# Moving elementwise work between engines, reordering the start, and placing buffers on the other side, in a forward-and-backward long-convolution kernel

## The chip, the cores and the metric

The kernel runs on one core of one Trainium2 chip. The metric is device time in microseconds (us), lower is better. Quoted times are medians over the runs of one kernel. The profile is one execution of the same program; its span is about two microseconds shorter than the times.

Names used below: PE is TensorE (matmuls), PEld its weight loads, DVE is VectorE, ACT is ScalarE, POOL is GpSimd, SP is SyncE, whose queue issues almost all transfers here.

## The reference

Four residual layers over x of 2048 x 512 (bf16), A, B, A, B, with shared weights, and then the gradient of all of it.

```python
def _A_ref(q, k, v, shift_k, ssm_k, ssm_D):
    k_shift = sum of 4 shifted copies of k, each times a column of shift_k   # (abridged)
    kv = k_shift * v
    kv_f, kf_f = rfft(kv padded to 2S), rfft(ssm_k padded to 2S)             # (abridged)
    y = irfft(kv_f * kf_f)[:S] + kv * ssm_D                                  # (abridged)
    return q * y
def _B_ref(x, w1, b1, w2, b2):
    h = _gelu(jnp.einsum("bsd,df->bsf", x, w1) + b1)                          # F = 1376, tanh GELU
    return jnp.einsum("bsf,fd->bsd", h, w2) + b2
x = A_q
x = x + _A_ref(_layernorm(x), A_k, A_v, ...)
x = x + _B_ref(_layernorm(x), B_w1, ...)
x = x + _A_ref(_layernorm(x), A_k, A_v, ...)
x = x + _B_ref(_layernorm(x), B_w1, ...)
# outputs: x, and the ten gradients of x for grad_out
```

The convolution result y depends only on k, v and the filters, so it is computed once and used by both A layers.

## The kernel before

The Fourier transforms are matmuls with cosine and sine blocks that the kernel generates itself. Its stages, in order, are these:

1. Generate the forward blocks (Fmat) and the inverse blocks (Imat) and store them.
2. Transform the filter h, form k_shift and kv, transform kv, multiply the spectra ("plain"), and transform back to y.
3. The forward layers. The dense layer works through four slices of 512 rows, twice (two B layers), with 11 chunks of up to 128 hidden columns in each slice.
4. The backward layers, twice: dense backward, weight gradients (dw2, then dw1), then the layer-norm backward of layer A.
5. gd (the gradient of ssm_D), the transform of gy, two spectral products ("conj", "conj_untwist"), two inverse transforms (gkv, then gh), and last gk and gw, the gradients of k and of shift_k.

The parts that the change and the argument touch, with cuts marked `...`:

```python
# --- start (setup_conv)
    with tc.tile_pool(name="gen_work", bufs=1) as gen_work, tc.tile_pool(name="gen_stage", bufs=3) as stage:
        gen_forward_blocks(nc, tc, gen_work, consts, dims, fdest)
        ...  # 32 stores Fmat <- Fblk
        for b in range(HT):
            for qc, qs in ((Q_ICE, Q_ISE), (Q_ICO, Q_ISO)):
                ...  # generate a pair of inverse blocks (stc, sts), store both to Imat
    ...
        for t in range(NT):
            nc.sync.dma_start_transpose(out=hT[:, t, :], in_=h_ap[0:D, t * P:(t + 1) * P])
    ...  # transform of h, then:
        with nc.allow_non_contiguous_dma(reason="tiny weight transpose"):
            nc.sync.dma_start(out=dram.WT[:, :], in_=W_ap.rearrange("d j -> j d"))
    ...
            eng = nc.gpsimd if (t % 2 == 0) else nc.vector      # k_shift: every second tile on POOL
            for j in range(4):
                ...
                    eng.tensor_tensor(out=tmp, in0=kj, in1=Wbc16[:, j, :], op=ALU.mult)
                    eng.tensor_tensor(out=ks, in0=ks, in1=tmp, op=ALU.add)

# --- spectral products
                nc.vector.scalar_tensor_tensor(out=t1, in0=Ar, scalar=sc, in1=Br, op0=ALU.mult, op1=ALU.mult)
                ...  # three more like it, then two tensor_tensor

# --- dense forward, one chunk (line numbers as in the profile)
            nc.scalar.activation(out=u, in_=ps, func=ACT.Identity, bias=w.b1col[...], scale=1.0)      # L634
            nc.gpsimd.tensor_tensor(out=wsq, in0=u, in1=u, op=ALU.mult)                               # L637
            nc.vector.tensor_scalar(out=tt, in0=wsq, scalar1=..., scalar2=..., ...)                   # L639
            nc.vector.tensor_tensor(out=arg, in0=tt, in1=u, op=ALU.mult)                              # L642
            nc.scalar.activation(out=sg, in_=arg, func=ACT.Sigmoid)                                   # L644
            nc.vector.tensor_tensor(out=hT_sl[0:fcs, c, :], in0=u, in1=sg, op=ALU.mult)               # L645
            nc.vector.tensor_scalar(out=tt, in0=tt, scalar1=3.0, ...)                                 # L646
            nc.gpsimd.tensor_tensor(out=wsq, in0=tt, in1=u, op=ALU.mult)                              # L648
            nc.vector.tensor_scalar(out=arg, in0=sg, scalar1=-1.0, scalar2=1.0, ...)                  # L649
            nc.gpsimd.tensor_tensor(out=arg, in0=arg, in1=wsq, op=ALU.mult)                           # L651
            nc.vector.scalar_tensor_tensor(out=gp, in0=arg, scalar=1.0, in1=sg, ...)                  # L653

# --- backward, weight gradients: pools opened on the same side as everything else
    with tc.tile_pool(name="bb_hm", bufs=3) as hm_pool, tc.tile_pool(name="bb_ev", bufs=2) as evp, ...
        ...  # per layer h_tm is loaded twice, 2 x 16 tiles of 344 KB
    with tc.tile_pool(name="bb_gm", bufs=3) as gm_pool, tc.tile_pool(name="bb_nm", bufs=3) as nm_pool, \
            tc.tile_pool(name="bb_ev1", bufs=2) as evp, ...

# --- the end: gk and gw, after both inverse transforms
        for t in range(NT):
            ...
                    nc.any.tensor_tensor(out=tmp, in0=gksj, in1=Wbc[:, j, :], op=ALU.mult)     # tmp, acc, Wbc in f32
                    nc.any.tensor_tensor(out=acc, in0=acc, in1=tmp, op=ALU.add)
                nc.any.tensor_tensor(out=prod, in0=gksj, in1=kt, op=ALU.mult)
                nc.tensor.matmul(psw[j], lhsT=consts.onescol, rhs=prod, start=(t == 0), stop=(t == NT - 1))
        ...
            with nc.allow_non_contiguous_dma(reason="tiny transposed store"):
                ...  # out4 stored element by element
```

## Time and profile before

The time before was 2176.45 us (four runs, 2174.79 to 2178.35). First come lines of the page of the kernel before: busy time of an engine (share of the span) and its instructions, and then the span cut in 40 slices of 54 us, each digit the busy share in tenths. "DMA" is the mean busy share of the 16 transfer engines.

```profile
PE 1134.6 (52%) x4992; PEld 463.8 (21%) x4992; DVE 1370.4 (63%) x2698; ACT 577.5 (27%) x947; POOL 395.1 (18%) x336
...
PE   0028009391655535666797572796550393049742
DVE  8447331778999999999474008671017718994296
POOL 0000550000677727777100000000000000000000
DMA  5721440703111121111344673347773426132242
```

No engine is the limit of the whole program: VectorE is busy 63% of it. Each stage has a limit of its own, and the rows of digits show the stages. TensorE does nothing in slices 0 and 1, has a hole in slices 4 and 5 while POOL works, and more holes in slices 24, 30, 31, 33 and 34. VectorE is at nine tenths or more in slices 10 to 18 (the dense forward). The transfer row is at 6 to 7 where VectorE is nearly idle (slices 22, 23, and 27 to 29: the weight gradients).

**The start.** The timeline of the SP queue of the kernel before over its first 150 us; columns are start, duration, engine, line, operation, out<-in, count:

```profile
0.74 0.82 SPq L342 DMA_DIRECT2D WT_d<-in_A_shift_k_dram  x1
1.62 30.15 SPq L541 DMA_DIRECT2D w_sb<-in_B_w_dram  x1
31.82 28.34 SPq L544 DMA_DIRECT2D w_sb<-in_B_w_dram  x11
60.28 21.28 SPq L291 DMA_DIRECT2D Fmat<-Fblk  x32
...
124.40 20.78 SPq L306 DMA_TRANSPOSE hT<-in_A_ssm_k_dram  x16
```

WT is a transposed store of two-byte elements. The 12 loads of w_sb behind it take until 60.16 us, so the stores of Fmat begin at 60.28 us and the transposing loads of h only at 124.40. The Trainium skill, "DMA: Bandwidth & Descriptors", Rules for kernel authors, says that a non-contiguous last dimension is lowered to one descriptor per element; the trace agrees, for its transfer records hold 2048 of two bytes, one for each of the 512 x 4 elements, that begin between 2.3 and 36.6 us. Why the loads of w_sb then take until 60 us is not shown.

**VectorE beside POOL.** The timeline of the kernel before inside one dense slice (VectorE and POOL lines picked out, same columns; brackets hold the idle time before and what ended it):

```profile
577.09 0.41 DVE L645 TENSOR_TENSOR hT_sl<-g_u,g_s 128x512 bf16<-128x512 bf16 x1
577.25 1.26 POOL L648 TENSOR_TENSOR g_w<-g_t,g_u 128x512 bf16<-128x512 bf16 x1 [0.83 <-DVE g_t L646]
577.43 1.24 DVE L649 TENSOR_SCALAR g_arg<-g_s 128x512 bf16<-128x512 bf16 x1
578.59 0.28 DVE L639 TENSOR_SCALAR g_t<-g_w 128x512 bf16<-128x512 bf16 x1
578.81 1.15 POOL L651 TENSOR_TENSOR g_arg<-g_arg,g_w 128x512 bf16<-128x512 bf16 x1 [0.30 <-DVE g_arg L649]
578.90 1.34 DVE L642 TENSOR_TENSOR g_arg<-g_t,g_u 128x512 bf16<-128x512 bf16 x1
```

L645, begun while POOL is idle, takes 0.41 us. L649, begun 0.18 us after a POOL operation, takes 1.24 us and ends 0.16 us after it; L639, begun when POOL is idle, takes 0.28. L642, the same kind of operation as L645, begins under L651 and takes 1.34. The VectorE operations here that begin under a POOL operation thus last until it is over. The groups of instructions of the kernel before (line, engine, operation, tiles, count, then busy us and mean ns, then idle time before and what ended it) hold the mixture of both kinds:

```profile
L653 DVE SCALAR_TENSOR_TENSOR g_gp<-g_arg,g_s 128x512 bf16<-128x512 bf16 (+1 forms) x88 | 97.7, 1114 | 14.1 <-POOL g_arg L651 14.1
L642 DVE TENSOR_TENSOR g_arg<-g_t,g_u 128x512 bf16<-128x512 bf16 (+1 forms) x88 | 82.7, 943 | 2.5 <-DVE g_t L646 0.3
L649 DVE TENSOR_SCALAR g_arg<-g_s 128x512 bf16<-128x512 bf16 (+1 forms) x88 | 77.3, 879 | 0.0
```

So L642 costs 943 ns on average instead of some 420. The Trainium skill, "SBUF — State Buffer", Terms, calls the port pair of VectorE and GpSimd an exclusive lock, where the loser "fully blocks". The timeline agrees with that rather than with shared bandwidth.

**Stages by window.** Busy time of each engine in stretches of the kernel before: a dense forward slice's worth, the first dw stage, the layer-norm backward after it, and the second pair. Columns: window, length, then busy us (instructions) of PE, PEld, DVE, ACT, POOL, then the granted clock of PE, DMA share, GB/s.

```profile
550.00:585.00 35.00, 19.65 (x84) 8.08 (x84) 31.52 (x52) 15.99 (x25) 25.41 (x22) 0.77 0.14 49
1176.00:1316.00 140.00, 95.14 (x367) 35.09 (x366) 2.21 (x4) 8.30 (x15) 0.00 (x0) 0.86 0.70 216
1316.00:1374.00 58.00, 12.10 (x35) 3.00 (x34) 54.40 (x134) 35.05 (x70) 0.00 (x0) 0.53 0.24 73
1477.00:1634.00 157.00, 96.56 (x368) 35.05 (x368) 14.86 (x23) 0.00 (x0) 0.00 (x0) 0.83 0.73 219
1634.00:1706.00 72.00, 0.00 (x0) 0.00 (x0) 61.10 (x146) 23.69 (x48) 0.00 (x0) 0.50 0.32 67
```

In the dense slice VectorE is busy 31.5 of 35 us. In the weight gradients TensorE is busy 95 of 140 us, the transfers 70%, and VectorE 2 us. Then VectorE is the busy engine, in the layer-norm backward: 54 of 58 us, and 61 of 72, with ScalarE at 35 and 24 us and TensorE at 12 and 0.

### The profile page before, as it was taken

How to read it: one execution, taken by the hardware profiler on the slowest of the kernel's cores; microseconds unless marked ns; L12 is line 12 of the kernel's file. 1: busy time of each engine (PE TensorE's matmuls, PEld its weight loads, DVE VectorE, ACT ScalarE, POOL GpSimd, SP SyncE). 2: the span in 40 equal slices, each digit the busy share in tenths (PEclk: the TensorE clock that was granted, in tenths of full speed). 3: DMA queues.
4: the chain of work that ended last, by engine and by line, in shares of the span. 5: the costliest groups of instructions: out<-in, count | busy, mean ns of one | idle time of the engine just before them, and what ended most of it. 6: DMA issues, size and time to landing. Idle time of an engine off the chain costs nothing.

```text
span 2175.8 us, 17475 instructions
## 1 busy us (share of the span) xinstructions
PE 1134.6 (52%) x4992; PEld 463.8 (21%) x4992; DVE 1370.4 (63%) x2698; ACT 577.5 (27%) x947; POOL 395.1 (18%) x336
## 2 busy tenths in 40 slices
PE   0028009391655535666797572796550393049742
PEld 0003004130222212222343220442220041014300
DVE  8447331778999999999474008671017718994296
ACT  8520003015455454333442005440003130001110
POOL 0000550000677727777100000000000000000000
PEclk9999559696767767666799886898885596569855
DMA  5721440703111121111344673347773426132242
GB/s 21 292 87 70 152 145 39 245 19 95 47 60 55 52 76 44 62 62 60 124 144 153 201 242 105 103 137 213 217 224 61 160 77 217 53 100 77 69 143 58
DMA packets 198639, 248.16 MB, mean 114 GB/s; under 512 B 35987, under 2 KB 146633, under 8 KB 197518
## 3 DMA queue, kind: packets, MB, share of 16 engines
q1 hardware_dynamic: 198542, 247.04, 36.8%
q8 instruction: 39, 0.64, 0.1%
q14 instruction: 58, 0.48, 0.1%
HBM read 152.24 MB, written 92.62 MB: 113 GB/s over the span
## 4 chain that ended last, share of the span: by engine, by line
DVE 41%; PE 27%; DMA 15%; issue 6%; POOL 4%; ACT 4%; SPq 3%; DVEq 0%; POOLq 0%; ACTq 0%
PE fwd_pss L179 4%; PE fwd_psc L176 4%; DVE g_gp L653 4%; PE gh_ps L785 3%; DMA dw_n<-n_d 3%; DVE g_arg L649 3%; DMA h_tm<-htm_d 3%; PE dw_ps L851 2%; DVE hT_sl L645 2%; PE dw_ps L822 2%; DMA sst<-Hspec_d 2%; PE inv_A L192 2%; DVE lb_junk L741 2%; PE inv_A L194 2%; DVE lb_tmp L747 2%
## 5 line engine op out<-in xcount | busy, mean ns | idle before, releaser
L660 PE MATMUL o_ps<-w_sb,hT_sl 128*128 128x512 bf16 (+1 forms) x352 | 136.1, 491 | 134.3 <-DVE hT_sl L645 132.6
L631 PE MATMUL z_ps<-nT,w_sb 128*128 128x512 bf16 (+1 forms) x352 | 134.0, 518 | 33.7 <-ACT g_u L634 33.1
L851 PE MATMUL dw_ps<-gz_tm,dw_n 128*128 128x512 bf16 (+1 forms) x384 | 96.3, 400 | 69.5 <-DMA dw_n<-n_d 62.9
L637 POOL TENSOR_TENSOR g_w<-g_u 128x512 bf16<-128x512 bf16 (+1 forms) x88 | 111.8, 1274 | 100.2 <-ACT g_u L634 96.1
L648 POOL TENSOR_TENSOR g_w<-g_t,g_u 128x512 bf16<-128x512 bf16 (+1 forms) x88 | 110.1, 1253 | 83.3 <-DVE g_t L646 80.1
L822 PE MATMUL dw_ps<-g_bf,h_tm 128*128 128x512 bf16 (+1 forms) x352 | 96.1, 419 | 41.8 <-DMA h_tm<-htm_d 30.0
L651 POOL TENSOR_TENSOR g_arg<-g_arg,g_w 128x512 bf16<-128x512 bf16 (+1 forms) x88 | 105.9, 1203 | 35.6 <-DVE g_arg L649 32.5
L653 DVE SCALAR_TENSOR_TENSOR g_gp<-g_arg,g_s 128x512 bf16<-128x512 bf16 (+1 forms) x88 | 97.7, 1114 | 14.1 <-POOL g_arg L651 14.1
L785 PE MATMUL gh_ps<-gT,w2T 128*128 128x512 bf16 (+1 forms) x352 | 88.8, 389 | 6.2 <-DVE gzT_sl L789 6.2
L634 ACT ACTIVATE g_u<-z_ps,b1col 128x512 bf16<-128x512 f32 (+1 forms) x88 | 59.8, 685 | 114.4 <-POOL g_w L648 81.3
L660 PEld LDWEIGHTS <-hT_sl 128*128 128x128 bf16 (+1 forms) x352 | 39.5, 115 | 227.2 <-DVE hT_sl L645 177.7
L644 ACT ACTIVATE g_s<-g_arg 128x512 bf16<-128x512 bf16 (+1 forms) x88 | 54.7, 627 | 111.7 <-DVE g_arg L642 111.0
L795 PE MATMUL gn_ps<-w1T,gzT_sl 128*128 128x512 bf16 (+1 forms) x352 | 84.2, 379 | 0.0
L642 DVE TENSOR_TENSOR g_arg<-g_t,g_u 128x512 bf16<-128x512 bf16 (+1 forms) x88 | 82.7, 943 | 2.5 <-DVE g_t L646 0.3
L789 DVE SCALAR_TENSOR_TENSOR gzT_sl<-gh_ps,gp_t 128x512 bf16<-128x512 f32 (+1 forms) x88 | 59.7, 688 | 35.1 <-PE gh_ps L785 28.0
L158 PE MATMUL rev_ps<-hT,anti 128*128 128x512 bf16 x8 | 3.7, 494 | 147.1 <-DMA hT<-in_A_ssm_k_dram 147.1
L649 DVE TENSOR_SCALAR g_arg<-g_s 128x512 bf16<-128x512 bf16 (+1 forms) x88 | 77.3, 879 | 0.0
L1126 PE MATMUL gw_ps<-gw_prod,onescol 128*1 128x512 bf16 x64 | 37.4, 585 | 72.2 <-DVE gw_prod L1125 72.2
L192 PE MATMUL inv_A<-P1spec,Iblk_b 128*128 128x512 bf16 x64 | 27.2, 424 | 83.6 <-ACT gk_a1s L1066 80.9
L379 ACT ACTIVATE KVspec<-fwd_psc 128x512 bf16<-128x512 f32 x16 | 9.4, 597 | 230.5 <-PE fwd_psc L176 230.5
L739 ACT ACTIVATE lb_j<-agn 128x512 bf16<-128x512 f32 x32 | 19.9, 623 | 177.0 <-DVE agn L880 176.9
L851 PEld LDWEIGHTS <-dw_n 128*128 128x128 bf16 x384 | 36.4, 106 | 129.5 <-DMA dw_n<-n_d 59.5
(272 smaller groups left out, 2814.2 us busy)
## 6 DMA issues: line engine op xcount, KB each, us to landing
h_tm<-htm_d SPq DMA_DIRECT2D x64, 344.0 KB, 3.4
gz_tm<-gztm_d SPq DMA_DIRECT2D x64, 344.0 KB, 4.2
htm_d<-h_tm SPq DMA_DIRECT2D x32, 344.0 KB, 2.3
gztm_d<-gz_tmj SPq DMA_DIRECT2D x32, 344.0 KB, 2.2
gp_d<-g_gp SPq DMA_DIRECT2D x80, 128.0 KB, 1.7
gp_t<-gp_d SPq DMA_DIRECT2D x80, 128.0 KB, 2.2
Fmat<-Fblk SPq DMA_DIRECT2D x32, 256.0 KB, 3.0
sst<-Hspec_d SPq DMA_DIRECT2D x64, 128.0 KB, 2.9
```

What stands on the lines that cost most here:

```text
L176: nc.tensor.matmul(psc, lhsT=blocks(qc, a)[:, b * P:(b + 1) * P], rhs=inc[a], start=(a == 0), stop=(a == HT - 1))
L179: nc.tensor.matmul(pss, lhsT=blocks(qs, a)[:, b * P:(b + 1) * P], rhs=ins[a], start=(a == 0), stop=(a == HT - 1))
L631: nc.tensor.matmul(ps[0:fcs, :], lhsT=w.w1[:, dc, f0:f0 + fcs], rhs=nT[:, dc, cols], start=(dc == 0), stop=(dc == ND - 1))
L637: nc.gpsimd.tensor_tensor(out=wsq[0:fcs], in0=u[0:fcs], in1=u[0:fcs], op=ALU.mult)
L648: nc.gpsimd.tensor_tensor(out=wsq[0:fcs], in0=tt[0:fcs], in1=u[0:fcs], op=ALU.mult)
L649: nc.vector.tensor_scalar(out=arg[0:fcs], in0=sg[0:fcs], scalar1=-1.0, scalar2=1.0, op0=ALU.mult, op1=ALU.add)
L651: nc.gpsimd.tensor_tensor(out=arg[0:fcs], in0=arg[0:fcs], in1=wsq[0:fcs], op=ALU.mult)
L653: nc.vector.scalar_tensor_tensor(out=gp[0:fcs], in0=arg[0:fcs], scalar=1.0, in1=sg[0:fcs], op0=ALU.add, op1=ALU.mult)
L660: nc.tensor.matmul(ps2, lhsT=hT_sl[0:fcs, c, ti * P:(ti + 1) * P], rhs=w.w2[0:fcs, c, :], start=(c == 0), stop=(c == NFC - 1))
L785: nc.tensor.matmul(ps[0:fcs, :], lhsT=bw.w2T[:, dc, f0:f0 + fcs], rhs=gT[:, dc, cols], start=(dc == 0), stop=(dc == ND - 1))
L822: nc.tensor.matmul(accs[c][0:fcs, :], lhsT=hm[:, f0:f0 + fcs], rhs=g_bf[:, t, :], start=(t == 0), stop=(t == NT - 1))
L851: nc.tensor.matmul(accs[(dc, fs0)][:, 0:fsz], lhsT=n_t[:, dc * P:(dc + 1) * P], rhs=gm[:, fs0:fs0 + fsz], start=(t == 0), stop=(t == NT - 1))
```

## The change

Its intent was to take elementwise work off POOL, use cheaper forms of VectorE operations, put the start in a better order, and let stages overlap that shared addresses. The core of the diff, with cuts marked:

```diff
@@ start @@
-        with nc.allow_non_contiguous_dma(reason="tiny weight transpose"):
-            nc.sync.dma_start(out=dram.WT[:, :], in_=W_ap.rearrange("d j -> j d"))
+    nc.sync.dma_start(out=Wsb, in_=W_ap.rearrange("(p c) j -> p c j", c=NC))
+    ...  # 16 small matmuls broadcast it into Wbc16; four rows of that are stored to WT
+    # order now: forward blocks, hT loads, transform of h, k_shift, then the inverse blocks, then kv
-            eng = nc.gpsimd if (t % 2 == 0) else nc.vector
+                eng = nc.vector
-        Hspec = hsp.tile([P, 4, HT, D], BF16, name="Hspec")      # stored whole after the transform
+            nc.sync.dma_start(out=dram.Hspec[qr, :, b, :], in_=hr)   # stored block by block
@@ spectral products: sign and scale moved out (2/L to the evacuation of the inverse transform) @@
-                nc.vector.scalar_tensor_tensor(out=t1, in0=Ar, scalar=sc, in1=Br, op0=ALU.mult, op1=ALU.mult)
+                te.tensor_tensor(out=t1, in0=Ar, in1=Br, op=ALU.mult)
 ...
@@ dense forward @@
-            nc.gpsimd.tensor_tensor(out=wsq[0:fcs], in0=u[0:fcs], in1=u[0:fcs], op=ALU.mult)
+            nc.scalar.activation(out=wsq[0:fcs], in_=u[0:fcs], func=ACT.Square)
-            nc.gpsimd.tensor_tensor(out=wsq[0:fcs], in0=tt[0:fcs], in1=u[0:fcs], op=ALU.mult)
-            nc.vector.tensor_scalar(out=arg[0:fcs], in0=sg[0:fcs], scalar1=-1.0, scalar2=1.0, ...)
-            nc.gpsimd.tensor_tensor(out=arg[0:fcs], in0=arg[0:fcs], in1=wsq[0:fcs], op=ALU.mult)
+            nc.vector.tensor_tensor(out=wsq[0:fcs], in0=tt[0:fcs], in1=u[0:fcs], op=ALU.mult)
+            nc.scalar.activation(out=oms[0:fcs], in_=sg[0:fcs], func=ACT.Identity, scale=-1.0, bias=...)
+            nc.vector.tensor_tensor(out=arg[0:fcs], in0=oms[0:fcs], in1=wsq[0:fcs], op=ALU.mult)
+            nc.vector.tensor_scalar(out=arg[0:fcs], in0=arg[0:fcs], scalar1=1.0, scalar2=None, op0=ALU.add)
-            nc.vector.scalar_tensor_tensor(out=gp[0:fcs], in0=arg[0:fcs], scalar=1.0, in1=sg[0:fcs], ...)
+            nc.vector.tensor_tensor(out=gp[0:fcs], in0=arg[0:fcs], in1=sg[0:fcs], op=ALU.mult)
@@ layer norms, gkv, gk: temporaries from F32 to BF16, nc.any to nc.vector @@
-        gn = pool.tile([P, D], F32, name="agn", tag="agn", bufs=3)
+        gn = pool.tile([P, D], BF16, name="agn", tag="agn", bufs=3)
 ...
@@ weight gradients: five pools @@
-    with tc.tile_pool(name="bb_hm", bufs=3) as hm_pool, tc.tile_pool(name="bb_ev", bufs=2) as evp, \
+    with tc.tile_pool(name="bb_hm", bufs=3, side="right") as hm_pool, \
+            tc.tile_pool(name="bb_ev", bufs=2, side="right") as evp, \
 ...
@@ tail: out4 by 16 tiny matmuls and one store instead of element stores @@
```

## The prediction

> **What bounds the kernel now.** No engine is busy throughout; stage by stage (windows table, 40 slices):
> - 0 to 449 us, setup to the first inverse transform. The queue of transfers is blocked to 60 us by the two-byte transposed weight store, so basis-block stores start only at 60; the Imat stores then pace the second generation, and hT lands at 144. PE runs h (163-212), then idles about 110 us while the shifted product runs on POOL/DVE (POOL 1.2 us per tile), then kv (335-388), then spectral products (DVE, 58 us).
> - 545-785 and 815-1048, forward dense layers: VectorE-bound (56 of 60 us), 59 us a slice. Six VectorE operations cost 4.5 us a chunk. While POOL works they are stretched: L642 0.94 us, L649 0.86, L653 1.15; uncontended in the timeline: 0.42, 0.28, 0.68. The Trainium skill, "GPSIMD Engine Reference", Key points, says that POOL shares SBUF interfaces with VectorE; these times agree.
> - 1165-1316 and 1470-1634, weight gradients: DMA-bound (share 0.64-0.73, DVE nearly idle). Then the layer-norm backward runs alone: 1316-1374 and 1634-1706, DVE busy 54 of 58 us; PE idle. Then gd, Fblk load, gy transform to 1797.
> - 1797-1935 spectral products, DVE-bound; 1935-2052 inverse transforms, PE-bound; 2052-2161 gk, DVE-bound (92 of 109).
>
> **What changes, and its worth.**
> 1. Start: transposed store gone, hT can load at once, inverse generation moved behind h and ks; ks all on VectorE (8 x 0.35 us x 16 = 45 us) inside h's shadow. Estimate: generation ends near 47, h on PE 47-105, kv near 140-200, first inverse near 245 instead of 449. Worth about 190.
> 2. Products: scalar_tensor_tensor (0.74 us bf16) becomes tensor_tensor (0.42 us here; the skill, "VectorE: DVE Perf Modes", tier table, gives bf16 tensor_tensor 2x). Start to start: plain included above; conj 3.5 to 2.1 us, untwist 5.0 to 3.7 us a block, 16 blocks each: about 40.
> 3. Dense forward: POOL emptied; VectorE per chunk 5 tensor_tensor x 0.35 + 3 tensor_scalar x 0.21 = 2.4 us; ACT gains Square and 1-s: four at 0.63-0.69 = 2.5 us. With epilogue about 34 us a slice on each; with ping-pong I take 40-42. 8 slices x 17.5 = about 140.
> 4. Layer norm forward in bf16: about 10.
> 5. Weight-gradient pools on the other side: first loads prefetch (9 us gap twice), and the layer-norm backward no longer shares addresses with those pools, so it hides beneath the DMA-bound stage, as do gd loads and part of the Fblk load. Gross 58+72+20; minus contention for the same DMA: net about 120.
> 6. gk: 11 tensor_tensor x 0.35 x 16 = 62 us instead of 104; tail without element stores: together about 40.
> Unchanged: transforms on PE, backward dense loops, DMA-bound weight gradients.
>
> Sum about 540: 2176 to 1636. I predict **1630 us**, range 1545 to 1730; chance of faster by over 2% 0.97, within 2% 0.02, slower 0.01.
>
> **What would show it.** POOL busy falls to a few us; mean of the L642 operation near 0.42 us; slices 38-44 us, ACT almost as busy as DVE there; PE's first h matmul near 50 us and no 110 us hole after it; layer-norm backward instructions inside the weight-gradient windows with no PE hole between layers; no sub-512-byte store at the start; gk stage about 65-70 us.
>
> **What would make it wrong.** ACT and VectorE handing work back and forth with two buffers (slices of 50 us); activation-table reloads for Square; the ordering not lifting layer-norm backward into the DMA-bound stage, or its loads slowing it; ks and h evacuation both on VectorE delaying kv; the PE clock, 0.65-0.79 now in the forward stage, staying low and making PE the limit; sst loads (3-4 us each, few buffers) limiting the faster products.

## The result

The time after is 1646.59 us (eight runs, 1643.83 to 1654.9), against 2179.49 us for the kernel before in the same rounds (13 runs). The ratio is 0.7559, with a 95% interval of 0.7546 to 0.7572. Ratios here and below are computed as the mean time of one kernel's fast runs over that of the other's of the same rounds, so they are not quite the ratio of the medians quoted. The prediction of 1630 us was 17 us too low, and its range held the result. All outputs are right.

The same lines of the page of the kernel after (slices of 41 us now):

```profile
PE 1080.4 (66%) x5024; PEld 447.9 (27%) x5024; DVE 1097.1 (67%) x3014; ACT 597.1 (36%) x1036; POOL 3.6 (0%) x16
...
PE   3672855907766477779975679955455865089944
DVE  8999746398999899838894018856513228973177
POOL 0000000000000000000000000000000000000000
DMA  5657566041222222344486754397786526241074
```

POOL is gone (3.6 us), VectorE has lost 273 us of busy time although it took over most of POOL's work, TensorE works from slice 0, and the long holes at the layer-norm backward are closed (those at the spectral products remain). Bytes moved were 248 MB in both; only their place changed.

The table sets the stages side by side; each row ends where the next begins. The markers are first starts read from the traces: y_lo (first inverse transform), z_ps (dense forward), the last o_ps, the first matmul of the gy transform that reads Fblk, the first pr_zr (untwist product), gk_lo, gw_prod.

| stage | ends, before | ends, after | length before | length after | change | predicted |
|---|---|---|---|---|---|---|
| start, to the first inverse transform | 449.5 | 280.2 | 449.5 | 280.2 | −169 | −190 |
| inverse transform, first layer A | 544.6 | 369.4 | 95.1 | 89.2 | −6 | −10 (layer norm) |
| dense forward, twice, with layer A between | 1046.4 | 696.6 | 501.8 | 327.2 | −175 | −140 |
| backward layers, gd, Fblk load | 1730.4 | 1273.4 | 684.0 | 576.8 | −107 | −120 |
| gy transform and conj product | 1854.1 | 1383.8 | 123.7 | 110.4 | −13 | −40 with the next |
| untwist product | 1935.1 | 1445.3 | 81.0 | 61.5 | −20 | |
| inverse transforms gkv, gh | 2062.7 | 1570.8 | 127.6 | 125.5 | −2 | 0 |
| gk, gw, tail | 2175.8 | 1642.7 | 113.1 | 71.9 | −41 | −40 |
| sum | | | 2175.8 | 1642.7 | −533 | −540 |

**The start after.** The timeline of the SP queue of the kernel after:

```profile
0.74 0.38 SPq L301 DMA_DIRECT2D Wsb<-in_A_shift_k_dram  x1
1.65 20.78 SPq L320 DMA_TRANSPOSE hT<-in_A_ssm_k_dram  x16
```

The loads of h go out at 1.65 us instead of 124.40. What is left of the hole is seen in the waits of TensorE between 110 and 180 us (first column: engine, tile, line, releaser; then us in total, times, longest):

```profile
PE rev_ps L160 <- DVE kvt L371: 40.1, 1, 40.1
```

In the kernel before, between 200 and 330 us, the same wait was this:

```profile
PE rev_ps L158 <- DVE kvt L371: 109.9, 1, 109.9
```

So 70 of the 169 us that the start gained are a shorter wait for kvt: k_shift now runs beside the transform of h and not behind it. In the window ahead of what is left of the wait, 47 to 153 us, VectorE is busy 102.6 of 106 us (first row; same columns as the windows above):

```profile
47.00:153.00 106.00, 55.67 (x235) 23.03 (x233) 102.56 (x219) 23.10 (x22) 0.00 (x0) 0.74 0.63 202
405.00:440.00 35.00, 25.89 (x127) 10.51 (x127) 34.70 (x110) 33.01 (x55) 0.00 (x0) 0.95 0.23 81
818.00:968.00 150.00, 96.10 (x379) 35.13 (x377) 60.02 (x159) 31.55 (x70) 0.00 (x0) 0.86 0.76 237
1066.00:1255.00 189.00, 97.53 (x376) 36.52 (x374) 82.39 (x197) 12.28 (x35) 0.00 (x0) 0.80 0.81 212
```

The other three rows of that view are a stretch of the dense forward (VectorE 34.7 and ScalarE 33.0 of 35 us, where they had 31.5 and 16.0) and the two dw stages. Into these has come VectorE work, 60.0 and 82.4 us in place of 2.2 and 14.9. That is the layer-norm backward, which now runs under them. The DMA share is larger (0.76 and 0.81 instead of 0.70 and 0.73). The windows of the two kernels do not end at the same point of the work, so their lengths aren't to be compared: from the first to the last dw matmul, the first stage took 140.7 us before and 141.4 after, the second 147.3 and 179.2.

The groups of the kernel after that answer to those of before:

```profile
L658 ACT ACTIVATE g_oms<-g_s,onescol_f 128x512 bf16<-128x512 bf16 x80 | 56.6, 713 | 0.4
L650 DVE TENSOR_TENSOR g_arg<-g_t,g_u 128x512 bf16<-128x512 bf16 x80 | 33.5, 421 | 1.1
L663 DVE TENSOR_TENSOR g_gp<-g_arg,g_s 128x512 bf16<-128x512 bf16 x80 | 33.4, 419 | 0.2
L656 DVE TENSOR_TENSOR g_w<-g_t,g_u 128x512 bf16<-128x512 bf16 x80 | 33.4, 419 | 0.0
```

L650 is the old L642: 421 ns instead of 943. L656 is POOL's L648, now 419 ns on VectorE. L663 is the old L653, a two-input operation instead of a three-input one: 419 ns, where it took 1114 beside POOL.

### The profile page after: what moved, and what is told of

The parts are those of the page before. It is cut to its first block, busy times and chain, and to the rows that moved or that the text cites. A ratio compares the mean times of both kernels' runs of the same rounds, so it can differ in the third digit from the quotient of the medians.

```text
span 1642.7 us, 17398 instructions
## 1 busy us (share of the span) xinstructions
PE 1080.4 (66%) x5024; PEld 447.9 (27%) x5024; DVE 1097.1 (67%) x3014; ACT 597.1 (36%) x1036; POOL 3.6 (0%) x16
## 4 chain that ended last, share of the span: by engine, by line
PE 34%; DVE 32%; DMA 20%; ACT 8%; issue 4%; SPq 1%; DVEq 0%; ACTq 0%
DMA h_tm<-htm_d 5%; PE fwd_psc L178 4%; PE fwd_pss L181 4%; DMA dw_n<-n_d 4%; PE gh_ps L794 4%; PE dw_ps L862 3%; DMA sst<-Hspec_d 3%; PE inv_A L194 2%; PE inv_A L202 2%; PE inv_A L196 2%; PE inv_A L200 2%; PE dw_ps L832 2%; PE gn_ps L804 2%; DVE bnst L534 2%; DVE g_arg L650 2%
## 5 line engine op out<-in xcount | busy, mean ns | idle before, releaser
L669 PE MATMUL o_ps<-w_sb,hT_sl 128*128 128x512 bf16 (+1 forms) x352 | 108.9, 413 | 52.6 <-DVE hT_sl L653 52.2
L832 PE MATMUL dw_ps<-g_bf,h_tm 128*128 128x512 bf16 (+1 forms) x352 | 95.1, 417 | 57.8 <-DMA h_tm<-htm_d 51.7
L639 PE MATMUL z_ps<-nT,w_sb 128*128 128x512 bf16 (+1 forms) x352 | 100.8, 414 | 13.0 <-ACT g_u L642 9.4
L669 PEld LDWEIGHTS <-hT_sl 128*128 128x128 bf16 (+1 forms) x352 | 34.9, 103 | 119.9 <-DVE hT_sl L653 85.8
L832 PEld LDWEIGHTS <-h_tm 128*128 128x128 bf16 (+1 forms) x352 | 34.2, 107 | 117.8 <-DMA h_tm<-htm_d 75.0
L744 ACT ACTIVATE lb_gn<-gn_ps 128x512 bf16<-128x512 f32 x32 | 19.1, 597 | 125.4 <-PE gn_ps L804 114.1
L658 ACT ACTIVATE g_oms<-g_s,onescol_f 128x512 bf16<-128x512 bf16 (+1 forms) x88 | 62.3, 713 | 0.4
L748 ACT ACTIVATE lb_j<-agn 128x512 bf16<-128x512 bf16 x32 | 20.1, 629 | 115.9 <-DVE agn L891 115.9
L629 PE MATMUL tr_ps<-ident,b_n 128*128 128x128 bf16 x128 | 16.5, 271 | 66.4 <-ACT b_n L624 46.8
L642 ACT ACTIVATE g_u<-z_ps,b1col 128x512 bf16<-128x512 f32 (+1 forms) x88 | 59.1, 678 | 2.5 <-PE z_ps L639 1.1
L1009 ACT ACTIVATE GYspec<-fwd_psc 128x512 bf16<-128x512 f32 x16 | 9.6, 597 | 132.5 <-DMA Fblk_b<-Fmat 106.1
L645 ACT ACTIVATE g_w<-g_u 128x512 bf16<-128x512 bf16 (+1 forms) x88 | 54.0, 621 | 1.8 <-DVE g_arg L660 1.5
L639 PEld LDWEIGHTS <-w_sb 128*128 128x128 bf16 (+1 forms) x352 | 36.6, 106 | 56.8 <-issue 38.0
```

Of the source, the lines that this page charges most:

```text
L639: nc.tensor.matmul(ps[0:fcs, :], lhsT=w.w1[:, dc, f0:f0 + fcs], rhs=nT[:, dc, cols], start=(dc == 0), stop=(dc == ND - 1))
L642: nc.scalar.activation(out=u[0:fcs], in_=ps[0:fcs], func=ACT.Identity, bias=w.b1col[0:fcs, c:c + 1], scale=1.0)
L658: nc.scalar.activation(out=oms[0:fcs], in_=sg[0:fcs], func=ACT.Identity, scale=-1.0, bias=consts.onescol_f[0:fcs, :])
L669: nc.tensor.matmul(ps2, lhsT=hT_sl[0:fcs, c, ti * P:(ti + 1) * P], rhs=w.w2[0:fcs, c, :], start=(c == 0), stop=(c == NFC - 1))
L832: nc.tensor.matmul(accs[c][0:fcs, :], lhsT=hm[:, f0:f0 + fcs], rhs=g_bf[:, t, :], start=(t == 0), stop=(t == NT - 1))
```

## The experiments

A name beginning with b_ is an edit of the kernel before, a_ of the kernel after, and v_ is an attempt at a faster kernel than both. The four groups of runs had 2173.79, 2169.6, 2178.56 and 2172.78 us for the kernel before.

### b_dve: only POOL's three operations of the dense chunk moved to VectorE

```diff
-            nc.gpsimd.tensor_tensor(out=wsq[0:fcs], in0=u[0:fcs], in1=u[0:fcs], op=ALU.mult)
+            nc.vector.tensor_tensor(out=wsq[0:fcs], in0=u[0:fcs], in1=u[0:fcs], op=ALU.mult)
 ...  (the same for L648 and L651)
```

> The kernel before, with the three POOL operations of the dense layer (u*u, t*u, (1-s)*w) issued on VectorE and nothing else changed, so VectorE has nine operations a chunk instead of six and ScalarE no more than before. Theory (POOL's two-input operations lock VectorE out of SBUF, so that VectorE's own operations are stretched): the stretched ones fall back to 0.42 us (L642), 0.28 us (L649) and 0.68 us (L653); VectorE needs about 6 x 0.35 us less, a chunk costs 5 x 0.35 + 3 x 0.21 + 0.68 = about 3.1 us, a slice about 40 to 42 us instead of 59, total 2030 to 2060 us. Rival (no contention; VectorE is simply full and POOL was real help): a slice grows by 11 x 3 x 0.35 = 11.6 us, total about 2270 us.

Measured: 2028.1 us, ratio 0.9329 (0.9308 to 0.935). VectorE got three more operations per chunk, it was the stage's busiest engine, and the stage became faster. From the first z_ps to the last o_ps it now takes 361 us (538.7 to 899.9) instead of 502. The groups of this kernel in that stretch:

```profile
L653 DVE SCALAR_TENSOR_TENSOR g_gp<-g_arg,g_s 128x512 bf16<-128x512 bf16 x80 | 54.8, 685 | 0.1
L642 DVE TENSOR_TENSOR g_arg<-g_t,g_u 128x512 bf16<-128x512 bf16 x79 | 33.1, 419 | 0.0
L649 DVE TENSOR_SCALAR g_arg<-g_s 128x512 bf16<-128x512 bf16 x80 | 23.0, 287 | 0.0
```

L642 fell from 943 to 419 ns, L649 from 879 to 287 and L653 from 1114 to 685 by POOL's silence alone. So contention is shown as the cause of the stretched times, and taking the three operations off POOL as worth about 141 of the 175 us that the dense forward gained. Not all of the 141 need be stretched operations: in that stage of the kernel before VectorE also stood waiting 18.5 us for results of POOL (14.1 at L653, 4.4 at L639), which this edit removes as well. The remaining 34 us (361 to 327) do not lie where one would look, in the cheaper chunk of the kernel after. From the first L642 (L650) of a slice to that of the next it took 34.4, 42.6 and 32.1 us in this kernel's first dense layer and 32.8, 42.9 and 32.0 in its second, 36 on average, and 36.2, 36.4, 37.9, 36.2, 33.0 and 31.5 us in the kernel after, 35 on average. In the kernel before it took about 56. So inside the slices nearly the whole gain comes with taking POOL out. Of the 34 us, 22 lie between the layers (from the last slice of the first layer to the first of the second: 95.8 us here, 74.0 in the kernel after), 6 in the slices and 7 behind the last one. Which part of the change brought these, no run separates.

### b_right: only the five weight-gradient pools put on the other side

```diff
-    with tc.tile_pool(name="bb_hm", bufs=3) as hm_pool, tc.tile_pool(name="bb_ev", bufs=2) as evp, \
+    with tc.tile_pool(name="bb_hm", bufs=3, side="right") as hm_pool, tc.tile_pool(name="bb_ev", bufs=2, side="right") as evp, \
 ...  (the same for bb_gm, bb_nm, bb_ev1)
```

> The kernel before, with only the weight-gradient pools placed on the other side of the memory (five pools). Theory (the layer-norm backward waited only because its tiles shared addresses with those pools): the layer-norm backward runs inside the weight-gradient windows, the first weight-gradient matmul follows the last gn matmul within 1 us instead of 8 us; total about 2180 - 100 to -120 = 2060 to 2080 us. Rival (what shortened that part was the bf16 arithmetic and the VectorE-only layer norm, not the placement): the layer-norm backward stays alone in its own windows and the total falls by less than 25 us.

Measured: 2060.95 us, ratio 0.9483 (0.9463 to 0.9503). One argument on five pools is worth 113 us. From the last o_ps to the first matmul of the gy transform it takes 572.9 us, where the kernel before has 684.0 and the kernel after 576.8, so it accounts for the whole gain of that row of the table. The windows of the two dw stages of this kernel:

```profile
1167.00:1320.00 153.00, 98.84 (x409) 37.30 (x415) 61.61 (x147) 45.11 (x89) 0.00 (x0) 0.88 0.75 238
1402.00:1591.00 189.00, 108.81 (x444) 41.95 (x452) 88.90 (x202) 32.15 (x65) 0.00 (x0) 0.81 0.80 208
```

VectorE is busy 61.6 and 88.9 us inside the stages in which it had 2.2 and 14.9, and the first layer-norm backward operation (agn) starts at 1172.0 instead of 1316.5. The edit changes nothing but where tiles lie, so the place is what had kept it waiting. The reading that fits is that the layer-norm tiles had been given addresses that the weight-gradient tiles held until their stage ended. The first dw matmul now follows 0.4 us after the matmul ahead of it, where it was 7.9. From the first to the last dw matmul the first stage did not grow (140.7 us before, 138.5 here) and the second did (147.3 to 176.4), while the transfers' share rose to 0.75 and 0.80. That is the price of the overlap, and it is nearly the same in the kernel after (141.4 and 179.2).

### b_wt: only the transposed two-byte store replaced

```diff
-            nc.sync.dma_start(out=dram.WT[:, :], in_=W_ap.rearrange("d j -> j d"))
+        nc.sync.dma_start(out=Wsb, in_=W_ap.rearrange("(p c) j -> p c j", c=NC))
 ...  (16 small matmuls into Wbc16, four row stores to WT, as in the kernel after)
```

> The kernel before, with only the two-byte transposed store of the shift weights replaced by a contiguous load and 16 small matmuls. Theory (this store blocks the one queue of transfers for 60 us): the first Fmat store is issued before 15 us instead of at 60, hT lands 40 to 60 us earlier than 144, and the shifted product begins some us sooner too; total 2180 - 45 to -65 = 2115 to 2135 us. Rival (generation on ScalarE and VectorE is what the h transform waits for; the store only filled idle time): less than 20 us.

Measured: 2152.06 us, ratio 0.9903 (0.9884 to 0.9921), a gain of 22 us, about half of what was expected. Lines of the SP queue's timeline in this kernel over its first 30 us (half of the 32 stores of Fmat fall into them):

```profile
1.28 7.41 SPq L552 DMA_DIRECT2D w_sb<-in_B_w_dram  x11
8.80 21.34 SPq L291 DMA_DIRECT2D Fmat<-Fblk  x16
```

The longest wait of ScalarE in the kernel before, over the first 200 us:

```profile
ACT sts L132 <- DMA Imat<-sts: 22.5, 1, 22.5
```

The queue really is free 51 us earlier (Fmat at 8.80 instead of 60.28). But the loads of h stand behind the inverse blocks in the queue, and those are generated at 2.9 us a pair until about 100 us. The loads of h moved from 124.4 to 101.8 us, which is the 22.5 us that ScalarE had waited for a free staging tile and no longer waits. A queue that was blocked for 50 us was worth 22, because a second limit stood just behind it. The rest of the start's gain comes from the other edits there (the order, and k_shift off POOL); a_genfirst tests one part of them.

### a_left: the kernel after with the five pools back on the left

```diff
-    with tc.tile_pool(name="bb_hm", bufs=3, side="right") as hm_pool, \
+    with tc.tile_pool(name="bb_hm", bufs=3) as hm_pool, \
 ...  (the same for bb_ev, bb_gm, bb_nm, bb_ev1)
```

> The kernel after, with the five weight-gradient pools back on the left side. Theory of the placement: the layer-norm backward comes out from under the weight gradients, the time grows by 85 to 110 us to about 1735 to 1755 us, with the same stage lengths elsewhere. Rival (placement is unimportant once the layer norm is in bf16): grows by less than 25 us.

Measured: 1700.94 us, ratio 0.7824 (0.7809 to 0.784), so 54 us slower than the kernel after by the medians (58 by the ratios, since the two ran in different rounds). Both expectations missed. The second layer-norm backward came out of hiding (its last agn at 1302.0 us, 76 us after the last dw matmul), but the first stayed hidden:

```profile
L891 DVE TENSOR_TENSOR agn<-g_f,y_res x32: 681/684/692, 820.3 to 1302.0; 128x512 bf16<-128x512 f32 x32
```

The first start is 820.3 us, as in the kernel after (820.7). A reason can be worked out from the tile sizes: the layer-norm tiles of this pool need about 13 KB a partition with BF16 temporaries and about 19 KB with F32, and ahead of the weight-gradient pools lies the dead tile gT of 16 KB. In BF16 they fit into it, so they need none of the weight-gradient addresses.

### a_left_pad: the same, with a dummy tile of 8 KB ahead of the first layer-norm tiles

```diff
+        pad = ap2.tile([P, 4096], BF16, name="pad", bufs=1)
+        nc.vector.memset(pad[:, 0:2], 0.0)
```

> The kernel after with the five pools back on the left (1700.9 us, where only the second layer-norm backward came out from under the weight gradients) and in addition an 8 KB per partition dummy tile ahead of the tiles of the first layer-norm backward. Theory (that first one stayed hidden because its bf16 tiles, about 13 KB, fit into the addresses of a tile that is free early, 16 KB; in the kernel before, f32 tiles made it 19 KB): with the dummy it spills into the weight-gradient pools' addresses and runs alone again; total 1735 to 1755 us, second dense backward loop about 40 us later. Rival (it stayed hidden for another reason, such as bf16 speed or ordering): unchanged at 1698 to 1704 us.

Measured: 1739.09 us, ratio 0.8016 (0.7999 to 0.8034; two runs of one round). The dummy tile does nothing but push the others out of the 16 KB:

```profile
L891 DVE TENSOR_TENSOR agn<-g_f,y_res x32: 677/681/692, 959.6 to 1345.1; 128x512 bf16<-128x512 f32 x32
```

agn now starts at 959.6 us, after the first dw stage, and 38 us are lost on top of the 54 (by the medians). So the pools' side and the smaller tiles of the change do partly the same thing. Hiding both layer-norm stages is worth 92 us in the kernel after (1739.09 less 1646.59), and the halved temporaries alone hide the first of them.

### a_genfirst: the kernel after, inverse blocks generated ahead of h again

```diff
+    for b in range(HT):                 # directly behind the forward blocks and their stores
+        for qc, qs in ((Q_ICE, Q_ISE), (Q_ICO, Q_ISO)):
+            ...                         # generate and store a pair of inverse blocks
 ...  (hT, transform of h, k_shift)
-        for b in range(HT):
-            for qc, qs in ((Q_ICE, Q_ISE), (Q_ICO, Q_ISO)):
-                ...
```

> The kernel after, with the generation of the inverse blocks put back ahead of the h transform in program order; everything else as after. The run with only the transposed store removed gained 22 us and left generation (2.9 us a pair, 32 pairs) as what h waits for. Theory (the rest of the early gain comes from taking 16 pairs of generation out of h's way): h's first evacuation moves from 61 us to about 100 us and the first inverse transform from 280 us by 20 to 45 us later; total 1667 to 1692 us. Rival (program order does not matter here because VectorE is full from 47 to 153 us whatever comes first, and the same generation work is then absent later): within 8 us of after.

Measured: 1660.58 us, ratio 0.7652 (0.7636 to 0.7669), 14 us slower than the kernel after by the medians and 20 by the ratios, and less than the 1667 us expected at least. The first y_lo moved by 22 us (280.2 to 302.2). The mechanism was a little off: the first evacuation of h did not move (61.3 and 62.0 us), but the last one did (114.1 to 135.0), and the last kvt did (152.7 to 183.7). The generation does not come first even when it is written first, because it interleaves with h; it takes VectorE time from a stretch in which VectorE is the limit. By the medians some of the 22 us are missing at the end, because the backward part (last o_ps to the gy transform) took 569.6 us here and 576.8 in the kernel after. But it took 570.8 and 570.4 in a_stt and a_oms of the same rounds, which leave it untouched as well, so this belongs to the rounds and not to the edit, and the 20 us by the ratios are the better figure.

### a_stt: the kernel after, products as three-input operations again

```diff
-                te.tensor_tensor(out=t1, in0=Ar, in1=Br, op=ALU.mult)
+                nc.vector.scalar_tensor_tensor(out=t1, in0=Ar, scalar=1.0, in1=Br, op0=ALU.mult, op1=ALU.mult)
 ...  (the same for all four products of all three modes)
```

> The kernel after, with the 12 products of the spectral stage as scalar_tensor_tensor with a scalar of 1.0 instead of tensor_tensor. Theory (the instruction form alone sets the rate: 0.74 us against 0.42 us): each of 3 x 16 blocks takes 4 x 0.33 = 1.3 us longer on VectorE; in conj and untwist that shows in full (about 40 us), in plain, where loads of the inverse blocks end at about the same time, partly (5 to 15 us); total 1690 to 1705 us. Rival (the stage is limited by the 128 KB loads, 3 to 4 us each): within 10 us of after.

Measured: 1663.35 us, ratio 0.7665 (0.7647 to 0.7683): 17 us slower by the medians and 23 by the ratios, where 1690 to 1705 us had been expected. At 683 ns instead of 422 each, the 64 operations of a product take 16.7 us more. The untwist product shows all of it: 61.5 us from pr_zr to gk_lo in the kernel after, 77.6 here. The conj product shows over half: from the end of the gy transform to the first pr_zr it took 53.2 us instead of 43.8. (The first pr_zr came only 3.6 us later, because the backward part ahead of it was 6 us shorter, as in a_genfirst and a_oms.) The plain product shows little: the first y_lo came 2.6 us later. The windows of the kernel after over its conj and its untwist product say why:

```profile
1340.00:1381.00 41.00, 10.41 (x30) 2.96 (x30) 31.07 (x89) 0.60 (x1) 0.00 (x0) 0.66 0.78 248
1384.00:1445.00 61.00, 8.53 (x31) 3.27 (x31) 61.00 (x160) 0.32 (x1) 0.00 (x0) 0.58 0.27 81
```

And the window of a_stt over its conj product:

```profile
1334.00:1387.00 53.00, 21.00 (x67) 7.42 (x67) 47.72 (x94) 0.60 (x1) 0.00 (x0) 0.65 0.70 228
```

In the conj product of the kernel after (first of the three rows) VectorE is busy 31 of 41 us and the transfers 78%: the spectra of h and the inverse blocks are being loaded, and a part of the slower products still fits; in a_stt VectorE is busy 47.7 of 53 us (third row). In untwist (second row) VectorE is busy all of 61 us, and there each operation counts. The operations cost 683 ns here as three-input and some 420 ns as two-input ones. The Trainium skill, "VectorE: DVE Perf Modes", The perf-mode tier table, gives two-input BF16 operations the 2x rate. Here they are 1.6 times as fast as F32 ones (420 ns against 680), which agrees in kind. The page has no row for the three-input form.

### a_oms: the kernel after, 1−s back from ScalarE to VectorE

```diff
-            nc.scalar.activation(out=oms[0:fcs], in_=sg[0:fcs], func=ACT.Identity, scale=-1.0,
-                                 bias=consts.onescol_f[0:fcs, :])
+            nc.vector.tensor_scalar(out=oms[0:fcs], in0=sg[0:fcs], scalar1=-1.0, scalar2=1.0, op0=ALU.mult,
+                                    op1=ALU.add)
```

> The kernel after, with only 1 - s of the dense layer moved from ScalarE back to VectorE as a tensor_scalar (about 0.21 us a chunk more on VectorE, 0.65 us less on ScalarE). After has both engines busy 33 to 35 of 35 us in a slice. If VectorE is the limit: slices grow by 11 x 0.21 = 2.3 us to about 37, total +15 to +20 us. If ScalarE, or the handing back and forth between the two, is the limit: slices shrink to 30 to 34 us, total -8 to -35 us. I hold the first more likely.

Measured: 1643.05 us, ratio 0.7561 (0.7533 to 0.7589): no difference, which neither theory expected. The operation is cheaper on VectorE (287 ns instead of 713), VectorE stays full (34.9 to 35.0 of 35 us) and ScalarE falls to 27.4 of 35. Meanwhile the copies that are left to any engine changed sides: of the copies of h_tm, 15 ran on VectorE in the kernel after and 6 here, and 58 instead of 49 on ScalarE. The dense forward as a whole took 331.6 us instead of 327.2: its slices 34.5 us on average instead of 35.2, the step from the first layer to the second 81.2 instead of 74.0. So a part of the load moved back by itself, and the test cannot tell which of the two engines limited the slice. That stays open.

### v_hact: the kernel after, two of four evacuation operations of h on ScalarE

```diff
-            nc.vector.tensor_scalar(out=a1, in0=pss, scalar1=scl, scalar2=None, op0=ALU.mult)
+            nc.scalar.activation(out=a1, in_=pss, func=ACT.Identity, scale=scl)
 ...  (the same for b1)
```

> The kernel after, with two of the four evacuation operations of the h transform (a1 and b1, a copy out of PSUM times a column) on ScalarE, which is busy only 12 of 50 and 8 of 50 us between 50 and 150 us there. Theory (from 47 to 153 us VectorE is the limit: h evacuation 48 us and the shifted product 53 us together, which is why kv began later than predicted): VectorE gets rid of 32 operations, 24 us by their busy time and about 22 by start-to-start; the last kvt moves from 153 us to 131 to 138, total 1622 to 1634 us. Rival (loads of k or generation on ScalarE set the pace there): within 6 us of after, or slower because generation shares ScalarE.

Measured: 1627.69 us, ratio 0.7475 (0.7457 to 0.7494), 19 us faster than the kernel after. The last kvt comes at 133.4 us instead of 152.7 and y_lo at 262.3 instead of 280.2. So VectorE was the limit of the start up to the last kvt.

### v_gk: the kernel after, gk made able to overlap the gh transform

```diff
-    p1p = ctx.enter_context(tc.tile_pool(name="cb_p1spec", bufs=1))
+    p1stack = ExitStack()                 # closed after the gkv transform
+            tc.tile_pool(name="gk_w", bufs=2, side="right") as gw, \
+            tc.tile_pool(name="gk_io", bufs=4, side="right") as io, \
-        psw = [gps.tile([1, D], F32, ...) for j in range(4)]
+        psw = gps.tile([4, D], F32, ...)      # one bank; the row is selected by a 128 x 4 selector
```

> The kernel after, with the gk stage allowed beneath the last inverse transform: its pools on the other side, open together with those of that transform, and its four column sums gathered in one PSUM bank by a 128x4 selector instead of four banks. After runs the transform on PE with VectorE busy 8 of 50 us (1500 to 1550) and then gk on VectorE with PE idle for 67 us. Theory (only addresses and banks kept them apart, as with the layer-norm backward): transform and gk together take about 80 to 95 us instead of 140; total 1585 to 1605 us. Rival (gk's loads of what the stage before has just stored, or ordering by priority, keep it behind): less than 15 us.

Measured: 1634.21 us, ratio 0.7496 (0.7483 to 0.751), 12 us faster, where 1585 to 1605 us had been expected. The addresses and the PSUM banks were free, gk's first product came 64 us earlier (1506.3), and yet the last came only 9 us earlier (1628.4). One wait of SP in this kernel tells why:

```profile
SPq L1128 <- DVE gw_prod L1136: 49.6, 2, 49.3
```

For 49.3 us the loads of gks stand still: a loaded tile is free when its product gw_prod has been made, and the products wait because the four gw_prod tiles are full. Their reader is a matmul that is written behind the whole inverse transform, and TensorE kept nearly to the written order: the first gw matmul ran at 1562.0 us, though its product had been made at 1506.3, and the last matmul of the transform at 1563.7. The rival (order, not addresses) held.

### v_all: four changes to the kernel after together

It takes v_hact, v_gk, the four column multiplications of untwist on ScalarE, and the load of Fblk written ahead of gd, so that it can start under the dw1 stage. The two edits not shown yet:

```diff
-                nc.vector.tensor_scalar(out=u1, in0=zs, scalar1=scl, scalar2=None, op0=ALU.mult)
-                nc.vector.scalar_tensor_tensor(out=out[:, qr, b, :], in0=zr, scalar=ccol, in1=u1, ...)
+                nc.scalar.activation(out=u1, in_=zs, func=ACT.Identity, scale=scl)
+                nc.scalar.activation(out=v1, in_=zr, func=ACT.Identity, scale=ccol)
+                te.tensor_tensor(out=out[:, qr, b, :], in0=v1, in1=u1, op=ALU.subtract)
 ...  (the same for u2, v2)
-    with tc.tile_pool(name="gd_w", bufs=3) as gw, ...   # gd, ahead of the Fblk load
 ...  (Fblk load, gy transform)
+    ...                                                 # gd, written behind the gy transform
```

> The kernel after with both changes above, and two more: in the untwisted product the four multiplications by a column go to ScalarE (idle there), which leaves VectorE eight tensor_tensor a block, 2.8 us instead of 3.8; and the load of the forward blocks for the gy transform comes before the gd products, which move beneath that transform. Sum of single expectations: 18 us (start), 50 (gk), 16 (untwist), 10 to 15 (gd and load; the load now competes with the DMA-bound weight gradients). Total 1540 to 1565 us. If the load's contention eats its gain, 1555 to 1570.

Measured: 1579.26 us, ratio 0.7248 (0.723 to 0.7266). This is above what was expected. The Fblk loads went out at 1189.1 to 1238.4 us, beginning 25 us before the last dw matmul (1214.3); in the kernel after they went out at 1269.2 to 1288.6, beginning 24 us after it (1245.5). From the last dw matmul to the end of the gy transform it took 75 us instead of 94. Untwist took 44 us instead of 61.5, but conj beside the loads took 54 instead of 44. What fell short was gk, for the reason that v_gk had shown.

### v_all2: v_all with gk's tiles written inside the steps of the inverse transform

```diff
             store_gh(a, lo, False)
             store_gh(NT - 1 - a, hi, True)
+            gk_tile(2 * a)          # the loop body of gk, tiles in descending order
+            gk_tile(2 * a + 1)
```

> v_all with one part mended: the key gradient's tiles are no longer written after the last inverse transform but two of them inside each of its eight steps (in descending order, so that the tile with the memsets comes first), so that the in-order TensorE meets a gw matmul soon after its product is ready and the four gw_prod buffers do not fill. Theory (what held v_gk and v_all back was TensorE's order): the stretch from the first gk_lo to the end, 188 us in v_all, holds 75 us of VectorE work and 97 us of TensorE work (some 20 of it only because the clock was granted at half) after the last gk_lo; run together it should take 85 to 110 us after the last gk_lo instead of 136. Time 1525 to 1555 us. First gw matmul some 12 us after the first inverse step, the SP wait on gw_prod (49 us in v_gk) gone, granted clock near 1 there. Rival (the part is limited by the loads of gks or by VectorE, and the order does not matter): 1570 to 1580 us. Everything ahead of the last gk_lo as in v_all, within 3 us.

Measured: 1539.03 us (five runs, 1537.85 to 1542.84), ratio 0.7093 (0.7079 to 0.7107), 40 us faster than v_all by the medians and 34 by the ratios, in the expected range. Two windows of v_all after the last gk_lo (columns as in the windows above):

```profile
1470.00:1505.00 35.00, 34.67 (x179) 15.06 (x183) 8.45 (x16) 8.23 (x14) 0.00 (x0) 1.00 0.02 6
1505.00:1540.00 35.00, 18.50 (x33) 2.63 (x32) 30.32 (x91) 0.00 (x0) 0.00 (x0) 0.56 0.80 253
```

And two windows of v_all2 in the same stage:

```profile
1460.00:1495.00 35.00, 34.84 (x160) 12.84 (x163) 30.65 (x86) 5.11 (x9) 0.00 (x0) 1.00 0.54 162
1495.00:1536.00 41.00, 32.96 (x163) 12.99 (x164) 30.22 (x80) 6.36 (x11) 0.00 (x0) 0.94 0.46 154
```

In v_all first TensorE works alone (34.7 of 35 us, VectorE 8.5) and then VectorE alone (30.3, TensorE 18.5 at a granted clock of 0.56). In v_all2 both are busy at once and the clock is 0.94 to 1.00. From the last gk_lo to the end it takes 101 us instead of 136. The wait on the full gw_prod tiles shrank to 12.5 us in 13 pieces. The Trainium skill, "TensorE: Matmul & The Clock Gate", Part 1: The HAM clock gate, says that the clock is halved when the array is left idle; the 0.56 beside sparse matmuls and the 1.00 beside dense ones agree. The same gw matmul took 547 ns on average in v_all and 384 in v_all2.

This is the fastest kernel: 108 us below the kernel after by the medians, and 634 below the kernel before in its own rounds.

## Why the prediction was right

**What bounds the kernel: right.** The stages and their limits were read from the windows and the waits, and b_dve, b_right and b_wt each moved the stage that they were aimed at, b_wt by half of what was expected. Two listed risks did not come: ScalarE's loads of function tables fell from 23 to 17, none of them at the line of Square, and the clock in the dense forward rose (0.77 to 0.95 in the windows shown).

**The dense forward (−140 predicted, −175 measured): mechanism right, size too small.** "With epilogue about 34 us a slice on each; with ping-pong I take 40-42." A slice takes 35 us, in which VectorE is busy 34.7 and ScalarE 33.0 of every 35, so the allowance for handing work back and forth was not needed: two buffers per tile were enough. The time of a slice before was also misread, as 59 us where the trace has 56 (the time ahead of the first slice and behind the last one of each layer had been divided over the four). Eight times 56 less 35 is 168 of the 175. b_dve shows that 141 of the 175 come with taking three operations off POOL, most of it contention. The predicted sum of 34 us a slice was nearly right, but the slices of b_dve, at 36 us with nothing moved to ScalarE, show that the work moved there was not what mattered.

**The start (−190 predicted, −169 measured): one term mis-sized.** The prediction put k_shift on VectorE "inside h's shadow". But the evacuation of h runs on VectorE too. Between 47 and 153 us it needs 47.6 us for h, 52.7 for k_shift and kv, and some generation, and is busy 102.6 of 106 us (the records of successive VectorE operations overlap by some 0.08 us, so their times add up to more). There was no shadow. TensorE waited 40 us for kvt. The prediction had listed this under what could make it wrong. v_hact confirmed it by taking 24 us off VectorE and gaining 19. This is not the whole miss: against "kv near 140-200, first inverse near 245" the kv transform ran from 153 to 228 us and the first inverse came at 280, so 13 us of the delay lie ahead of kv and 22 in it and behind it, where no run looked. Nor is the whole gain tested: of the 169 us, b_wt reproduces 20 (its first y_lo comes at 429.9), and a_genfirst loses 22; what the rest owes to k_shift on VectorE and what to its place beside h, no run separates.

**The backward part (−120 predicted, −107 measured): one step wrong.** The layer-norm backward hid beneath the weight gradients, as said, and b_right and a_left_pad show that addresses had kept it out. But the prediction had "part of the Fblk load" hidden as well. In the kernel after, Fblk is loaded directly after gd, at 1269.2 to 1288.6 us, with TensorE idle, just as before (1726.1). Its pool is opened after gd's pool is closed; in v_all, where it is opened first, the loads begin 25 us ahead of the last dw matmul instead of 24 us behind it. That gd's freed addresses caused it is the likely reading, but v_all changed the order in which they are written as well, so the two aren't told apart. The allowance for contention (150 less 120, so 30) was about right: from first to last matmul the dw stages grew by 33 us together (288 to 321), all of it in the second.

**The products (about −40 predicted, −33 measured): half right.** Untwist gave 20 us, as costed (5.0 to 3.7 us a block is 21 us over 16 blocks). In conj the change of 1.4 us a block (22 us over 16) could not come out whole, for there the loads limit; the gy transform and conj together gave 13. a_stt shows the same: slowing the products cost 16 us in untwist and 9 in conj. The prediction had named the loads as a risk.

**gk and tail (−40 predicted, −41 measured): right.** First to last gw_prod took 66.4 us instead of 96.0, and the tail from the last gw_prod to the end 5.5 instead of 17.1.

**Layer norm (−10 predicted, −6 measured).** The stage includes the inverse transform, so this is only a bound; it was not tested alone.

The errors of the terms, +35 and −21, −13, −7, −4, +1, nearly cancel. That is luck: the total was better than its parts.

## What to carry to other kernels

Read a VectorE operation's duration beside what POOL does at that moment before handing POOL "free" work: three operations per chunk on POOL cost the busiest engine more than doing them itself. If a stage waits for an engine that is idle and data that is there, look at the addresses its tiles were given, and at what stands ahead of it in that engine's program; v_gk and v_all2 had the same work, and only the second could overlap it. When one blocked resource is freed, look for the limit standing right behind it before costing the gain: the blocked queue gave 22 us, though it was free 51 us earlier.

## What the Trainium skill lacked or had wrong

- "VectorE: DVE Perf Modes" (The perf-mode tier table) has no row for the three-input operation (scalar_tensor_tensor). On 128x512 BF16 tiles it took 683 ns with a constant and 743 with a column as its scalar, against 419 for the two-input one. In this program that was worth 17 us by the medians and 23 by the ratios (a_stt).
- "SBUF — State Buffer" (Terms) says that the loser of the shared ports fully blocks. That agrees with the timeline here, but no page says what it costs a real program: VectorE operations of 287 and 419 ns averaged 879 and 943, and taking three of nine operations off POOL saved 146 us of 2174 (b_dve).
- "GPSIMD Engine Reference" (Key points) puts VectorE at about twice GpSimd's rate for elementwise work. Here a two-input BF16 operation took 1152 ns on GpSimd (median of L651, 1147 at least) and 419 on VectorE, 2.7 times.
- No page tells of whole stages that wait for one another because of the addresses of their tiles. Here it was worth 113 us (b_right), and 8 KB of an unused tile cost 38 us (a_left_pad against a_left).
- "DMA: Bandwidth & Descriptors" (Rules for kernel authors) warns of non-contiguous last dimensions, but gives no figure for what one costs the loads behind it in the queue: here 51 us of the queue, of which the program felt 22 (b_wt).
